# Layer one's twelve weight-pair blocks all by seven products, with low halves and column sums allowed on GpSimd, in a fused attention and two-layer MLP kernel

## The chip, the cores and the metric

The kernel runs on one core of a Trainium2 chip. The metric is device time in microseconds (us) of one execution; lower is better. The kernel before took 608.57 us (median of 3 runs, 606.79 to 608.82).

## The reference

Everything is float32. An attention (batch 2, 8 heads, 768 positions, head size 64; each position sees the last 96 positions and the first 8, with a bias that falls linearly with distance) gives 1536 tokens of 512 numbers. Two MLP layers follow:

```
x = attention(q, k, v)                       # 1536 x 512
h = x @ w_in;  r = max(h, 0);  g = s*r*r + b;  x = g @ w_out      # layer one, 512 -> 2048 -> 512
h = x @ w_in2; r = max(h, 0);  g = r*r;        out = g @ w_out2   # layer two
```

The weights arrive as 64-bit floats and are decoded on the chip.

## The kernel before, in words

**Precision.** A float32 operand is split into a high half (rounded to the fp32r format, on ScalarE or GpSimd: `whi`, `wsh`, `gh`, `tsh`, `zsh`) and a low half, which is the operand minus its high half (a two-input subtract, on VectorE: `wlo`, `wsl`, `gl`, `tsl`, `zsl`, lines 441, 475, 612, 615, 523). A product takes three matmuls: high by high, high by low, low by high.

**Blocks.** The hidden width 2048 is cut into 16 chunks of 128 in each layer. The first four chunks of layer one (`h` L695, `y` L774, 256 tokens at a time) are interleaved with the attention. All other chunks are worked in pairs (a, a+1): six pairs in layer one (4 to 14) and eight in layer two (16 to 30), each for two token halves tp of 768, so twelve blocks in layer one and sixteen in layer two. A pair of weight chunks by a token half is a 2 x 2 block product. Either it is done plainly (`plain` L549: 4 results x 4 row blocks x 3 = 48 matmuls of 384 columns), or by seven products in Winograd's form (`product` L538: 7 x 2 x 3 = 42 matmuls). `PLAIN` lists the blocks done plainly: pairs 4 and 6, both halves.

**What seven products need beside the matmuls.** For each pair of weight chunks, four sums of weight blocks (`ws` L458) and their split (`wshi`, `wslo` L475). For each token half, four column sums T1 to T4 for two row blocks kt (`tsum1` L517 in layer one, `tsum` L504 in layer two), each split by `tsplit` (high L221 or L225, low L523). They are worked one after the other, T3, T1, T2, T4 for kt 0 and then for kt 1, in one buffer of tag `tq`; layer two's use the buffer `m1`, which also holds the copy of a block's first product (`mid`). T1 overwrites a part of X, so it waits until the first four chunks, and the plain blocks, have read it. For each block, VectorE adds the products together: `mid` u2 and u3 (L559) and three `cadd` (L572), from PSUM. The products run in the order of `STAGES`: A11*B11, S2*T2, A12*B21, S3*T3, S1*T1, A22*T4, S4*B22.

**From layer one to layer two.** Layer one's output is summed in `acc` (`flush` L781, `flush2` L664). Because g is made as sign(s) times its value (`sg`), `acc` is multiplied by `sg` at the end by four ScalarE instructions a token half (`flush2` part 1, through `copy_r` L221), and only then split and summed in columns for layer two.

**Order.** `order` lists every task with the engines that may run it, a planned duration, what it depends on, its place in the rings of buffers and a due time `key`, to which `SHIFT` adds. `Plan.run` then walks through time and gives each engine the ready task with the least key. That fixes the instruction order of every engine and the choice of engine where several are allowed ("DVX" is a VectorE task that also uses the port shared with GpSimd). On the chip every engine works through its own queue in that order and waits on semaphores. Where TensorE has no ready task before the first `h`, the plan puts in a small matmul on zeros (`warm` L324).

In layer two the first product of a block waits for all eight column sums and the three splits of the token half, in layer one for all eight column sums (`dt`, added to stage 0 alone).

Of the kernel before, what the change touches and what calls it, by code (L numbers as in the profile page):

```python
# [19 lines left out]
P = 128  # L20
# [10 lines left out]
PLAIN = ((4, 0), (6, 0), (4, 1), (6, 1))  # L31
# [27 lines left out]
def decoded(a):  # L59
# [9 lines left out]
SHIFT = {('at', 0, 0): -17.4, ('at', 2, 0): 83.2, ('at', 2, 3): -18.5, ('at', 3, 0): 18.1, ('at', 6, 0): -32.5,  # L69
    ('at', 8, 0): -19.9, ('at', 8, 1): -18.7, ('cadd', 16, 0, 1, 0): 13.9, ('cadd', 24, 0, 1, 1): 64, ('cadd', 8, 0,  # L70
# [28 lines left out]
    0): -49.2, ('qk', 9, 0): -21.3, ('relu', 0, 0): 113.3, ('relu', 0, 256): 15.4, ('relu', 1, 0): -19.6, ('relu',  # L99
# [21 lines left out]
class Plan:  # L121
# [13 lines left out]
    def run(self, lat, patience):  # L135
# [92 lines left out]
class Fast:  # L228
# [269 lines left out]
    def tsum(self, tp, kt, step):  # L498
        b = [self.part(tp, x)[:, kt] for x in range(4)]
        if step % 3 == 0:  # L500
            self.T["t", tp, kt] = self.tm.tile([P, SB], F32, tag="m1", name=f"t{step}_{tp}_{kt}")
# [852 lines left out]
```

## Time and profile before

| what | value |
|---|---|
| median of 3 runs | 608.57 us (606.79 to 608.82) |
| the profiled execution's own time | 606.85 us |
| its span, first to last instruction | 605.1 us |
| granted TensorE clock, mean | 0.999 |

How to read the profile: PE is TensorE's matmuls, PEld its weight loads, DVE VectorE, ACT ScalarE, POOL GpSimd. A matmul's recorded length includes its run through the array, so matmuls overlap; the distance from one start to the next is what one costs. A row of the timeline has: start us, length us, engine, line, operation, output<-input, shapes, how many were merged, and in brackets the idle time before it with what ended it. A row of the instruction groups has: count, then busy us and mean ns of one, then idle time before them with what ended it. A row of the windows has: the stretch, its length, then busy us and count for PE, PEld, DVE, ACT and POOL, the granted clock, the DMA share and GB/s. A row of the waits has: total us, times, longest.

### The profile page before, as it was taken

How to read it: one execution, taken by the hardware profiler on the slowest of the kernel's cores; microseconds unless marked ns; L12 is line 12 of the kernel's file. 1: busy time of each engine (PE TensorE's matmuls, PEld its weight loads, DVE VectorE, ACT ScalarE, POOL GpSimd, SP SyncE). 2: the span in 40 equal slices, each digit the busy share in tenths (PEclk: the TensorE clock that was granted, in tenths of full speed). 3: DMA queues.
4: the chain of work that ended last, by engine and by line, in shares of the span. 5: the costliest groups of instructions: out<-in, count | busy, mean ns of one | idle time of the engine just before them, and what ended most of it. 6: DMA issues, size and time to landing. Idle time of an engine off the chain costs nothing.

```text
span 605.1 us, 10174 instructions
## 1 busy us (share of the span) xinstructions
PE 591.4 (98%) x3705; PEld 533.9 (88%) x3705; DVE 496.8 (82%) x1115; ACT 354.5 (59%) x774; POOL 113.7 (19%) x187
## 2 busy tenths in 40 slices
PE   8999999999999999999999899999999999999995
PEld 5788898999999999999999788899899999899984
DVE  7999898877999799987989999989587978774452
ACT  7999897756754445544667585655354645434330
POOL 5464432101112111111201012213010111000000
PEclk9999999999999999999999999999999999999999
DMA  7775641022321200312130302241222122000023
GB/s 283 286 268 182 218 157 39 3 96 73 111 70 36 80 26 1 110 61 74 51 124 1 104 2 70 69 140 35 70 69 90 51 69 71 35 1 1 0 106 109
DMA packets 14889, 52.11 MB, mean 86 GB/s; under 512 B 1904, under 2 KB 2160, under 8 KB 14832
## 3 DMA queue, kind: packets, MB, share of 16 engines
q1 hardware_dynamic: 14832, 51.39, 25.2%
q8 instruction: 31, 0.51, 0.3%
q14 instruction: 26, 0.21, 0.1%
HBM read 48.24 MB, written 3.15 MB: 85 GB/s over the span
## 4 chain that ended last, share of the span: by engine, by line


## 5 line engine op out<-in xcount | busy, mean ns | idle before, releaser
L538 PE MATMUL h<-xh,u 128*128 128x384 f32 x384 | 111.7, 337 | 1.2 <-ACT m L221 1.2
L641 PE MATMUL yy<-u,gh 128*128 128x512 f32 x360 | 111.8, 392 | 0.0
L635 PE MATMUL yy<-gh,u 128*128 128x512 f32 (+1 forms) x384 | 97.7, 337 | 0.2 <-ACT gh L605 0.2
L538 PE MATMUL h<-th,u 128*128 128x384 f32 x288 | 85.6, 338 | 0.0
L641 PEld LDWEIGHTS yy<-u,gh 128*128 128x128 f32 x360 | 67.2, 188 | 11.8
L635 PEld LDWEIGHTS yy<-gh,u 128*128 128x128 f32 x384 | 66.8, 189 | 8.5 <-ACT gh L605 0.5
L225 POOL TENSOR_SCALAR u<-st 128x512 fp32r<-128x512 f32 (+1 forms) x47 | 35.2, 749 | 202.4 <-PE h L538 58.7
L538 PEld LDWEIGHTS h<-xh,u 128*128 128x128 f32 x384 | 70.5, 188 | 2.6 <-ACT m L221 1.5
L641 PE MATMUL yy<-u,gl 128*128 128x512 f32 x180 | 70.4, 391 | 0.7 <-DVE gl L615 0.7
L635 PE MATMUL yy<-gl,u 128*128 128x512 f32 (+1 forms) x192 | 64.9, 338 | 1.8 <-DVE gl L612 1.8
L538 PE MATMUL h<-xl,u 128*128 128x384 f32 x192 | 64.6, 337 | 0.0
L538 PEld LDWEIGHTS h<-th,u 128*128 128x128 f32 x288 | 53.1, 188 | 1.9 <-DVE u L559 0.4
L221 ACT ACTIVATE u<-st 128x512 fp32r<-128x512 f32 (+1 forms) x41 | 26.2, 639 | 44.6 <-PE h L538 13.4
L221 ACT ACTIVATE st<-st 128x512 f32<-128x512 f32 x64 | 42.8, 676 | 11.7 <-DMA st<-in_moe_w_in_dram 8.0
L52 DVE SCALAR_TENSOR_TENSOR st<-st 128x512 int32<-128x512 int32 x64 | 46.1, 723 | 3.7 <-ACT st L221 0.9
L538 PE MATMUL h<-tl,u 128*128 128x384 f32 x144 | 48.5, 337 | 0.0
L375 ACT ACTIVATE sn<-sn,nm 128x256 f32<-128x256 f32 (+1 forms) x96 | 46.0, 483 | 1.4 <-DVE nm L367 1.3
L55 DVE SCALAR_TENSOR_TENSOR st<-st 128x512 int32<-128x512 int32 x64 | 44.8, 700 | 0.9
L594 ACT ACTIVATE r<-r 128x384 f32<-128x384 f32 x64 | 33.6, 526 | 13.6 <-DVE r L589 9.0
L635 PEld LDWEIGHTS yy<-gl,u 128*128 128x128 f32 x192 | 36.3, 189 | 5.9 <-DVE gl L612 2.1
L641 PEld LDWEIGHTS yy<-u,gl 128*128 128x128 f32 x180 | 33.8, 188 | 8.5 <-DVE gl L615 1.1
L585 ACT ACTIVATE u<-u 128x384 f32<-128x384 f32 x32 | 16.7, 522 | 37.6 <-DVE u L572 37.5
(153 smaller groups left out, 1308.9 us busy)
## 6 DMA issues: line engine op xcount, KB each, us to landing
st<-in_moe_w_in_dram SPq DMA_DIRECT2D x32, 512.0 KB, 3.9
st<-in_moe_w_out_dram SPq DMA_DIRECT2D x32, 512.0 KB, 3.6
q<-in_qk_dram SPq DMA_DIRECT2D x10, 768.0 KB, 5.0
v<-in_v_dram SPq DMA_DIRECT2D x10, 512.0 KB, 4.6
out_dram<-acc SPq DMA_DIRECT2D x11, 256.0 KB, 2.3
q<-in_qk_dram SPq DMA_DIRECT2D x2, 512.0 KB, 5.0
v<-in_v_dram SPq DMA_DIRECT2D x2, 256.0 KB, 6.0
out_dram<-acc SPq DMA_DIRECT2D x2, 128.0 KB, 3.1
```

Source lines behind the costliest of these rows:

```text
L52: nc.vector.scalar_tensor_tensor(out=lo, in0=hi, scalar=3, in1=lo, op0=ALU.logical_shift_left, op1=ALU.bitwise_or)
L55: nc.vector.scalar_tensor_tensor(out=lo, in0=hi, scalar=-(1 << 31), in1=lo, op0=ALU.bitwise_and, op1=ALU.bitwise_or)
L221: nc.scalar.activation(out=out, in_=in_, func=AF.Copy, scale=scale)
L225: nc.gpsimd.tensor_scalar(out=out, in0=in_, scalar1=scale, scalar2=0.0, op0=ALU.mult, op1=ALU.add)
L375: self.nc.scalar.activation(out=sn[:, x], in_=sn[:, x], func=AF.Exp, scale=-1.0, bias=self.nm[:, n, h:h + 1], accum_out=self.rs[:, n, h:h ...
L538: self.nc.tensor.matmul(ps, p, q, start=first and kt == 0 and x == 0, stop=kt == 1 and x == 2, skip_group_check=not first)
L585: nc.scalar.activation(out=r, in_=h, func=AF.Relu, scale=rt)
L594: nc.scalar.activation(out=r, in_=r, func=AF.Square)
L635: self.nc.tensor.matmul(yj, p[:, js], q[:, lo:hi], start=first and x == 0 and not (side and j % 2), stop=last and x == 2 and not (side and ...
L641: self.nc.tensor.matmul(y[m], p[:, ms], q, start=first and x == 0, stop=last and x == 2)
```

## The change

All blocks of layer one go by seven products (`PLAIN` is empty). The low halves of weights, of column sums and of layer two's g, and layer two's column sums themselves, may run on GpSimd beside VectorE. The sign is applied where layer one's results leave PSUM (`flush`, `flush2`), and the eight ScalarE instructions on `acc` go. Each product waits for the one column sum or split that it reads. Layer two's column sums use the buffer `tq`. The token half that is needed first gets its sums first. `SHIFT` has other values throughout, and a table `PIN` of 202 entries fixes a task's engine; the plan adds a cost when TensorE turns between kinds of work, and some planned durations change. The diff, with both tables cut to a few entries:

```diff
-PLAIN = ((4, 0), (6, 0), (4, 1), (6, 1))
+PLAIN = ()
...
-SHIFT = {('at', 0, 0): -17.4, ('at', 2, 0): 83.2, ('at', 2, 3): -18.5, ('at', 3, 0): 18.1, ('at', 6, 0): -32.5,
...
+SHIFT = {('at', 10, 3): 21.4, ('at', 2, 1): 59.4, ('at', 4, 0): 46.1, ('at', 4, 3): -15.5, ('at', 6, 1): -4.2,
...
+    ('lq', 2): -536.5, ('lq', 3): -435.9, ('lq', 4): -186.5, ('lq', 7): -193.6, ('lw', 0, 0): -5.9,
...
+PIN = {('at', 0, 0): 'ACT', ('at', 2, 0): 'ACT', ('at', 2, 1): 'DVE', ('at', 2, 3): 'DVE', ('at', 4, 0): 'ACT',
...
+TURN = ((0.0, 0.09, 0.18, 0.08), (0.095, 0.0, 0.095, 0.095), (0.095, 0.095, 0.0, 0.095), (-0.08, 0.09, 0.09, 0.0))
+KIND = {"qk": 1, "pv": 2, "tr": 3}
...
                     free[e] = now + engs[e]
+                    if e == "PE":
+                        k = KIND.get(self.tasks[t][0][0], 0)
+                        free[e] += TURN[kind][k]
+                        kind = k
...
-    def tsum(self, tp, kt, step):
+    def tsum(self, tp, kt, step, e):
...
-            self.T["t", tp, kt] = self.tm.tile([P, SB], F32, tag="m1", name=f"t{step}_{tp}_{kt}")
+            self.T["t", tp, kt] = self.tq.tile([P, SB], F32, tag="tq", name=f"t{step}_{tp}_{kt}")
...
-        self.nc.vector.tensor_tensor(out=t, in0=x, in1=y, op=ALU.subtract)
+        getattr(self.nc, e).tensor_tensor(out=t, in0=x, in1=y, op=ALU.subtract)
...
-            self.nc.vector.tensor_tensor(out=l, in0=t, in1=h.bitcast(F32), op=ALU.subtract)
+            getattr(self.nc, e).tensor_tensor(out=l, in0=t, in1=h.bitcast(F32), op=ALU.subtract)
...
-            nc.vector.tensor_tensor(out=gl, in0=r, in1=gh.bitcast(F32), op=ALU.subtract)
+            getattr(nc, e).tensor_tensor(out=gl, in0=r, in1=gh.bitcast(F32), op=ALU.subtract)
...
-                nc.vector.tensor_tensor(out=a, in0=y, in1=a, op=ALU.add)
-            elif part == 1:
-                a = accT[:, j, t0:t0 + TB]
-                copy_r(nc, e, a, a, self.sg)
+                nc.vector.scalar_tensor_tensor(out=a, in0=y, scalar=self.sg, in1=a, op0=ALU.mult, op1=ALU.add)
...
-            self.nc.vector.tensor_tensor(out=a, in0=y, in1=a, op=ALU.add)
-        else:
-            copy_r(self.nc, e, a, y)
+            self.nc.vector.scalar_tensor_tensor(out=a, in0=y, scalar=self.sg, in1=a, op0=ALU.mult, op1=ALU.add)
+        else:
+            copy_r(self.nc, e, a, y, self.sg)
...
+        if name in PIN:
+            engs = {e: d for e, d in engs.items() if e.replace("DVX", "DVE") == PIN[name]}
...
-        add(("wlo", w, i), "DVX:0.61", lambda e: f.wlo(w, i, e, v), [("whi", w, i)] + late(w, i, "l"), key,
+        add(("wlo", w, i), "DVX:0.61 POOL:1.25", lambda e: f.wlo(w, i, e, v), [("whi", w, i)] + late(w, i, "l"), key,
...
-            add(("wsl", what, a), "DVX:0.34" if small else "DVX:0.61",
+            add(("wsl", what, a), "DVX:0.34 POOL:0.75" if small else "DVX:0.61 POOL:1.25",
...
-    for tp in range(2):
+    tps = sorted(range(2), key=lambda tp: min((t for _, a, x, t in quads if x == tp and not plain(a, x)), default=0.0))
+    for tp in tps:
...
-                add(("zsl",) + v + (x,), "DVX:0.51", lambda e, v=v, x=x: f.tsplit(*v, x, 1, e),
+                add(("zsl",) + v + (x,), "DVX:0.51 POOL:1.0", lambda e, v=v, x=x: f.tsplit(*v, x, 1, e),
...
-        if not one:
-            dt = [("tsl", tp, kt, x) for kt in range(2) for x in range(4)] + [("xl", "x", tp, j) for j in (0, 2, 3)]
-        elif plain(a, tp):
-            dt = ["second"]
-        else:
-            dt = [("zsl", tp, kt, x) for kt in range(2) for x in range(4)]
         wino = not plain(a, tp)
+        tl = lambda x: [("zsl" if one else "tsl", tp, kt, x) for kt in range(2)]
+        xl = lambda j: ["second"] if one else [("xl", "x", tp, j)]
+        dt = (xl(0), tl(1), xl(2), tl(3), tl(0), tl(2), xl(3))
...
-                    [prev] + [("wsl", x, a) for x in need[s]] + extra[s] + dt * (s == 0), tm + 1.05 * s,
+                    [prev] + [("wsl", x, a) for x in need[s]] + extra[s] + dt[s], tm + 1.05 * s,
...
-            add(("gl",) + v, "DVX:0.56" if one else "DVX:0.49", lambda e, v=v: f.act(*v, "gl", e), [("gh",) + v], k,
+            add(("gl",) + v, "DVX:0.56" if one else "DVX:0.49 POOL:1.0", lambda e, v=v: f.act(*v, "gl", e), [("gh",) + v], k,
...
-            for j in range(4):
-                add(("sg", tp, j), "ACT:0.85", lambda e, g=g, tp=tp, j=j: f.flush2(g, tp, j, 1, e),
-                    [last[j], last[4 + j // 2]], k)
...
-                    add(("ts",) + v + (x,), "DVX:0.49", lambda e, v=v, x=x: f.tsum(*v, x),
+                    add(("ts",) + v + (x,), "DVX:0.49 POOL:1.0", lambda e, v=v, x=x: f.tsum(*v, x, e),
-                        sgn(kt) + [("tsl",) + v + (x - 1,)] * (x > 0) + [("tsl", tp, 0, 3)] * (kt > 0), k,
-                        acq=[("m1", "t") + v + (x,)] * new)
+                        acq=[("tq", "t") + v + (x,)] * new)
```

Of the 202 entries of `PIN`, 30 put a low half or a column sum on GpSimd (8 `wsl`, 7 `gl`, 7 `wlo`, 5 `zsl`, 1 `tsl`, 2 `ts`); tasks without an entry are left to the plan.

## Rows read from the trace of the kernel before

**Rows 1.** The page: the span, and busy time of each engine.
```profile
span 605.1 us, 10174 instructions
PE 591.4 (98%) x3705; PEld 533.9 (88%) x3705; DVE 496.8 (82%) x1115; ACT 354.5 (59%) x774; POOL 113.7 (19%) x187
```

**Rows 2.** The waits of PE, longest in total.
```profile
PE yy L635 <- DVE gl L612: 1.8, 1, 1.8
...
PE h L538 <- ACT m L221: 1.2, 1, 1.2
...
PE yy L641 <- DVE gl L615: 0.7, 1, 0.7
```

**Rows 3.** Windows: busy time by engine before, in and after layer one.
```profile
100.00:145.00 45.00, 44.91 (x421) 42.62 (x421) 35.88 (x104) 29.43 (x76) 7.50 (x13) 1.00 0.10 36
145.00:320.00 175.00, 175.00 (x1020) 164.15 (x1019) 154.80 (x282) 97.06 (x174) 24.64 (x33) 1.00 0.22 70
320.00:385.00 65.00, 61.12 (x321) 54.32 (x320) 63.31 (x117) 44.97 (x79) 9.91 (x13) 1.00 0.16 49
```

**Rows 4.** PE's timeline: plain blocks (L549), y (L774), seven products (L538).
```profile
145.22 0.34 PE L549 MATMUL h<-xh,u 128*128 128x384 f32 x1
...
153.66 0.28 PE L774 MATMUL y<-gh,u 128*128 128x256 f32 x1
...
157.96 0.34 PE L549 MATMUL h<-xh,u 128*128 128x384 f32 x1
...
162.12 0.28 PE L774 MATMUL y<-gh,u 128*128 128x256 f32 x1
...
163.55 0.34 PE L549 MATMUL h<-xh,u 128*128 128x384 f32 x1
...
304.09 0.34 PE L538 MATMUL h<-xh,u 128*128 128x384 f32 x1
...
308.26 0.39 PE L635 MATMUL yy<-gh,u 128*128 128x512 f32 x1
```

**Rows 5.** Instruction groups by line: what the change adds, takes out or moves.
```profile
L475 DVE TENSOR_TENSOR u<-st,u 128x512 fp32r<-128x512 f32 (+1 forms) x48 | 31.1, 665 | 4.5 <-PE yy L641 3.2 <-PE yy L635 0.9 <-ACT u L221 0.4
...
L441 DVE TENSOR_TENSOR u<-st,u 128x512 fp32r<-128x512 f32 x40 | 27.6, 693 | 5.5 <-PE yy L635 2.5 <-POOL u L225 2.0 <-ACT u L221 0.7
L572 DVE TENSOR_TENSOR u<-h,u 128x384 f32<-128x384 f32 x48 | 26.5, 553 | 13.1 <-PE h L538 12.8
L559 DVE TENSOR_TENSOR u<-h,m 128x384 f32<-128x384 f32 x48 | 26.5, 552 | 7.5 <-PE h L538 5.6 <-ACT st L221 1.7
...
L458 DVE TENSOR_TENSOR st<-st,st 128x256 f32<-128x256 f32 x36 | 16.4, 478 | 0.3
...
L221 ACT ACTIVATE acc<-acc,sg 128x768 f32<-128x768 f32 x8 | 7.2, 927 | 0.0
```

**Rows 6.** DVE's timeline: first instructions of column sums, layer one, first token half.
```profile
128.27 0.55 DVE L517 TENSOR_TENSOR tq<-xh 128x384 f32<-128x384 f32 x1
...
132.71 0.56 DVE L517 TENSOR_TENSOR tq<-xh 128x384 f32<-128x384 f32 x1
...
179.43 0.56 DVE L517 TENSOR_TENSOR tq<-xh 128x384 f32<-128x384 f32 x1
...
183.65 0.54 DVE L517 TENSOR_TENSOR tq<-xh 128x384 f32<-128x384 f32 x1
...
187.73 0.56 DVE L517 TENSOR_TENSOR tq<-xh,tq 128x384 f32<-128x384 f32 x1
...
190.74 0.55 DVE L517 TENSOR_TENSOR tq<-xh,tq 128x384 f32<-128x384 f32 x1
```

**Rows 7.** Timeline of POOL and of DVE where they meet.
```profile
334.85 0.98 POOL L225 TENSOR_SCALAR u<-st 128x512 fp32r<-128x512 f32 x1 [4.16 <-PE yy L635]
...
335.23 1.01 DVE L504 TENSOR_TENSOR t<-acc 128x384 f32<-128x384 f32 x1
```

**Rows 8.** Instruction group: the small matmuls on zeros in the first 25 us.
```profile
L324 PE MATMUL warm<-idle 128*128 128x256 bf16 x48 | 7.0, 283 | 0.0
```

More of the change, by code (lines that the diff above doesn't have):

```diff
@@ new lines @@
+SHIFT = {('at', 10, 3): 21.4, ('at', 2, 1): 59.4, ('at', 4, 0): 46.1, ('at', 4, 3): -15.5, ('at', 6, 1): -4.2,
+    ('at', 8, 2): 153.6, ('cadd', 12, 0, 1, 0): 116.6, ('cadd', 18, 0, 0, 1): 106.2, ('cadd', 18, 0, 1, 0): 42.9,
[19 rows of a table added]
+    ('norm', 11, 1): -157.2, ('norm', 11, 2): 52.7, ('norm', 3, 1): 18, ('norm', 5, 0): 14.2, ('norm', 8, 3): -3.9,
[5 rows of a table added]
+    0, 1024): 41.9, ('relu', 12, 0, 0, 1): 49.2, ('relu', 3, 1024): 156.6, ('relu', 3, 512): -24, ('relu', 4, 0, 0,
[3 rows of a table added]
+    9, 1): 82.4, ('ts', 0, 0, 2): -8.9, ('tsl', 0, 0, 1): -1.3, ('ttr', 3, 2): -31.7, ('ttr', 5, 0): 30.5, ('u2',
+    18, 1): 55.6, ('u2', 24, 0): 34.6, ('u2', 6, 0): -22.5, ('u2', 8, 1): 117.3, ('whi', 1, 0): 87.9, ('whi', 12,
+    1): 189.2, ('whi', 21, 1): 34.2, ('whi', 4, 1): -32.7, ('wlo', 19, 1): 28.4, ('wlo', 25, 1): 5.5, ('wlo', 26,
[3 rows of a table added]
+    ('wsh', 'S34', 6): 4.6, ('wsl', 'A1', 10): -72.6, ('wsl', 'A1', 20): 130.3, ('wsl', 'A1', 24): -1.6, ('wsl',
[9 rows of a table added]
@@ L146, in run @@
         held = {"DVE": 0.0, "POOL": 0.0}
+        kind = 0
         self.busy = dict.fromkeys(ready, 0.0)
@@ L823, in order @@
     plan.fill, plan.until = lambda: f.warm(0), ("h", 0, 0)
-    add("n", "SP:0.47", lambda e: None, key=-1000.0, dma=0.06)
+    add("n", "SP:1.2", lambda e: None, key=-1000.0, dma=0.06)
     add("nd0", "POOL:2.1", lambda e: f.consts(0), key=-60.0)
@@ L847, in order @@
                     dq.append(("tr", m, grp(m, mf)[0]))
-                add(("qk",) + u, {"PE": 1.07 if two else 1.17}, lambda e, u=u: f.qk(*u), dq, t, acq=[("a", "s", x) + u for x in range(2)],
+                add(("qk",) + u, {"PE": 0.97 if two else 1.1}, lambda e, u=u: f.qk(*u), dq, t, acq=[("a", "s", x) + u for x in range(2)],
                     rel=[("q", n)] * (hf or not two))
@@ L861, in order @@
                     lambda e, w=w: f.norm(*w, e), [("rs",) + u], t - 1)
-                add(("tr",) + w, {"PE": 0.45}, lambda e, w=w: f.tr(*w), [("norm",) + w], t - 2,
+                add(("tr",) + w, {"PE": 0.438}, lambda e, w=w: f.tr(*w), [("norm",) + w], t - 2,
                     acq=[("a", "t") + w], rel=[("sN",) + w])
@@ L867, in order @@
         t = vt[n, 1] + (cfg["att"] if two else -500.0)
-        add(("pv", n), {"PE": 1.9 if two else 1.1}, lambda e, n=n: f.pv(n), [("at", n, g) for g in grp(n, None)] + [("lv", n)],
+        add(("pv", n), {"PE": 1.8 if two else 1.0}, lambda e, n=n: f.pv(n), [("at", n, g) for g in grp(n, None)] + [("lv", n)],
             t - 3, acq=[("a", "o", n)], rel=[("at", n, g) for g in grp(n, None)] + [("v", n)])
@@ L976, in order @@
         tm, fin = t + cfg["moe"], lo == NT - 256
-        add(("h",) + u, {"PE": 1.44}, lambda e, u=u: f.h(*u, u[1] + 256), dh, tm, acq=[("h",) + u],
+        add(("h",) + u, {"PE": 1.43}, lambda e, u=u: f.h(*u, u[1] + 256), dh, tm, acq=[("h",) + u],
             rel=[slot(w, 0, x) for x in "hl"] * fin)
@@ L985, in order @@
         add(("gl",) + u, "DVX:0.42", lambda e, u=u: f.glo(*u, u[1] + 256), [("gh",) + u], t, rel=[("r",) + u])
-        add(("y",) + u, {"PE": 1.45}, lambda e, u=u, new=new, end=end: f.y(*u, new, end),
+        add(("y",) + u, {"PE": 1.435}, lambda e, u=u, new=new, end=end: f.y(*u, new, end),
             [("gl",) + u, ("wlo", w, 1)] + ([("y",) + before] if before else []) + last * new, tm + cfg["ylag"],
@@ L993, in order @@
                 more = lo in done
-                add(last[j], "DVE:0.6" if more else "DVE:0.6 ACT:0.48",
-                    lambda e, lo=lo, j=j, more=more: f.flush(lo, j, more, e), [("y",) + u], t)
+                add(last[j], "DVE:0.67" if more else "DVE:0.6 ACT:0.5",
+                    lambda e, lo=lo, j=j, more=more: f.flush(lo, j, more, e), [("y",) + u, ("root", 0)], t)
             done.add(lo)
     fin = {a: tp for _, a, tp, _ in quads}
-    for tp in range(2):
+    tps = sorted(range(2), key=lambda tp: min((t for _, a, x, t in quads if x == tp and not plain(a, x)), default=0.0))
+    for tp in tps:
         d0 = ["second"] + [("h", w, lo) for w in range(NF) for lo in range(tp * TB, tp * TB + TB, 256)]
@@ L1117, in order @@
                 df += [("xl", "x", k, x) for k in range(2) for x in (0, 2, 3)]
-            add(name, "DVE:0.6 ACT:0.48" if g[0] == NCH else "DVE:0.6",
+            add(name, "DVE:0.6 ACT:0.48" if g[0] == NCH else "DVE:0.67" if one else "DVE:0.6",
                 lambda e, g=g, tp=tp, j=j: f.flush2(g, tp, j, 0, e), df, tc + span + cfg["tk"])
@@ L1125, in order @@
             k = tc + span + cfg["tk"]
-            for j in range(4):
-                add(("sg", tp, j), "ACT:0.85", lambda e, g=g, tp=tp, j=j: f.flush2(g, tp, j, 1, e),
-                    [last[j], last[4 + j // 2]], k)
-            sgn = lambda kt: [("sg", tp, kt), ("sg", tp, kt + 2)]
             for j in (0, 2, 3):
+                r, c = divmod(j, 2)
                 add(("xh", "x", tp, j), "ACT:0.75", lambda e, g=g, tp=tp, j=j: f.flush2(g, tp, j, 2, e),
-                    [("sg", tp, j // 2 * 2), ("sg", tp, j // 2 * 2 + 1)], k)
-                add(("xl", "x", tp, j), "DVX:1.0", lambda e, g=g, tp=tp, j=j: f.flush2(g, tp, j, 3, e),
+                    [last[2 * r], last[2 * r + 1]] + [last[4 + r]] * c, k)
+                add(("xl", "x", tp, j), "DVX:1.03", lambda e, g=g, tp=tp, j=j: f.flush2(g, tp, j, 3, e),
                     [("xh", "x", tp, j)], k)
@@ L1138, in order @@
                     new = x % 3 == 0
[L1139 to L1141 removed]
+                    add(("ts",) + v + (x,), "DVX:0.49 POOL:1.0", lambda e, v=v, x=x: f.tsum(*v, x, e),
+                        [[last[kt], last[4]], [last[kt + 2], last[5]], [], []][x] + [("tsl",) + v + (x - 1,)] * (x > 0) +
+                        [("tsl", tp, 0, 3)] * (kt > 0), k,
+                        acq=[("tq", "t") + v + (x,)] * new)
                     add(("tsh",) + v + (x,), "ACT:0.44 POOL:0.6", lambda e, v=v, x=x: f.tsplit(*v, x, 0, e),
                         [("ts",) + v + (x,)], k)
[L1144 to L1145 removed]
+                    add(("tsl",) + v + (x,), "DVX:0.51 POOL:1.0", lambda e, v=v, x=x: f.tsplit(*v, x, 1, e),
+                        [("tsh",) + v + (x,)], k, rel=[("tq", "t") + v + (x // 3 * 3,)] * (x > 1))
     add("check", "DVE:2.0", lambda e: f.check(), ["second", ("relu", NF - 1, NT - 256)], use[6],
```

57 lines of the change are left out of this document (40 added, 17 removed), and 83 rows, old and new, of tables (PIN, SHIFT).

## The prediction

> **What bounds the kernel now.** I read the page's busy times first: TensorE is busy for 591.4 of 605.1 us, VectorE for 496.8, GpSimd for 113.7 [rows 1]. TensorE sets the time; the reader should see also that VectorE comes next and that GpSimd has room. Busy matmuls overlap, so I then took two other views. The list of TensorE's waits names three that matter, 1.8 + 1.2 + 0.7 = 3.7 us, all behind VectorE or ScalarE [rows 2]. The windows say where: TensorE is busy in all of 145 to 320 us (layer one's blocks), and loses 3.9 us in 320 to 385, the passage from layer one to layer two, where VectorE is busy for 63.3 of 65 us [rows 3]. In layer one VectorE works 154.8 of 175 us, just before it 35.9 of 45. So two things can shorten the kernel: fewer matmuls anywhere, and an earlier end of VectorE's work in the passage. One thing can lengthen it: more work on VectorE in layer one.
>
> The profiled execution took 606.85 us, 1.7 above its span and 1.7 (0.28%) below the median of the three runs, inside their spread. The sum starts from 606.85; 0.3%, about 1.8 us, is what a measurement of this kernel can tell from no change.
>
> **Part 1, four blocks by seven products.** A plain block's 48 matmuls run from 145.22 to 153.66, 0.176 us each; 24 matmuls of seven-product work run from 304.09 to 308.26, 0.174 each [rows 4]. A block loses six matmuls, so 4 x 6 x 0.174 = 4.2 us. TensorE has no idle time there to hide this, so it comes off the end in full: **-4.2**.
>
> What it adds goes to VectorE: per block two `mid` and three `cadd` at 0.55, 4 x 5 x 0.55 = 11.0 us; per weight pair four sums at 0.48, 2 x 4 x 0.48 = 3.8; four low halves at 0.665 in place of two at 0.693, 2 x 1.27 = 2.5 [rows 5]. Together 17.3 us. From 100 to 320 us VectorE works 190.7 of 220 [rows 3]; with the addition it would be 208 of 216, so it still fits, by 8 us, without any help. I cost it at nothing; the cover is these 8 us, and what comes late when they are gone is the low half (`gl`) for which `yy` waits, the wait of [rows 2]. High halves and copies for the new weight sums (some 2 to 4 us) go to ScalarE, idle 78 of 175 us there [rows 3].
>
> **Part 2, the column sums come earlier.** Their number stays, but until now the plain blocks ran first. The first sum starts at 128.27, once the attention is done [rows 6], and this floor stays. S2*T2 of the first block needs T1 for both kt, but the sums are made T3, T1, T2, T4, so it needs seven links of the chain. Links with three VectorE instructions took 4.44, 4.22 and 4.08 us to the start of the next, one with two took 3.01 [rows 6]: four at 4.2 and three at 3.0, the last without the gap to its successor (some 2.6), give 25.4, so T1 is there at about 153.7. TensorE's other work: the first block could start at 145.22, four `y` behind it (153.66 to 157.96 and 162.12 to 163.55, 5.7 us) can come first, and A11*B11 needs no sum (6 x 0.174 = 1.0) [rows 4]: enough until 152.0. So **+1.7**. Since TensorE takes its queue in order, all its later matmuls stand behind that wait. The bounds: nothing, if the links keep to their bare instructions or the new order ends the attention earlier; +7.4, if all seven take 4.44.
>
> **Part 3, the passage to layer two.** Eight multiplications by `sg` of 0.927 each leave ScalarE [rows 5], and the eviction multiplies instead, with the same operands plus one number per partition, so VectorE's count stays. A token half's sums no longer stand behind four of them. The column sums leave the buffer `m1`, for which the first product's copy waits (1.2 us of [rows 2]); the first product waits for one split in place of eight sums and three splits; some sums and low halves leave VectorE, on which the `gl` of the other two waits queued. I take 3.2 of the 3.7 us away, **-3.2**; the bounds are 0 (all stays) and 3.9 (the whole loss of the window).
>
> **Part 4, low halves on GpSimd.** No row shows GpSimd with two inputs. The nearest is its one-input split of 128 x 512 in 0.98 us, part of it spent against VectorE [rows 7]; the plan in the diff puts 1.25 on a low half. I take 1.25. Each one frees 0.67 us of VectorE. What it costs VectorE is seen where they meet: a two-input subtract of 128 x 384, 0.55 us elsewhere [rows 6], took 1.01 when it started 0.60 us before the end of GpSimd's split [rows 7]. It lost 0.46, all but 0.14 of what was left. Bounds for one low half: nothing lost, or 1.25 - 0.14 = 1.11. I take 0.45, the loss of that row, since instructions with an input in PSUM ran beside GpSimd's at a mean of 0.55 [rows 5]. Thirty low halves then free 30 x (0.67 - 0.45) = 6.6 us. This moves nothing on TensorE by itself: 0. GpSimd's queue grows by some 38 us of 605, but the high halves it also makes stand behind these longer instructions; whoever reads them waits up to 1.25 us more, and the weights are made well ahead of use.
>
> The Trainium skill, GPSIMD Engine Reference, section 3.1, states about 2.6 cycles an element for two inputs on GpSimd and advises VectorE for such work. An estimate from it is 512 x 2.6 / 1.2 GHz = 1.11 us plus dispatch, so the sum by the page would be that by the plan's 1.25; no run here shows it yet.
>
> **Part 5, the new order.** The loads of attention tiles 2 to 4 move far forward in SP's queue, ahead of weight loads. No transfer is added. In the first 25 us, 48 small matmuls, 7.0 us, fill TensorE's waiting [rows 8]: that bounds a gain; a loss could be as large. I take 0, as every operation of that chain stays. The cost for turning between kinds of work adds no instruction.
>
> **Sum.** 606.85 - 4.2 + 1.7 - 3.2 = 601.15, **601.2 us**, against 606.85, and 0.9 to 1.2% below the runs shown.
>
> **The rivals.** *A, the passage keeps its waits* (another VectorE instruction stands before `gl`): 606.85 - 4.2 + 1.7 = 604.4. For it: VectorE has 1.7 us of room in 65 there, and relief rests on GpSimd. Against: 7.4 us of ScalarE in that very chain go. *B, the first block waits for its sums at the slow pace*: 606.85 - 4.2 - 3.2 + 7.4 = 606.9, no change. For it: all of VectorE's added work begins just there. Against: VectorE has 9 us free from 100 to 145, and nothing fixes the attention's end at 128.
>
> *C, GpSimd stops VectorE, slower.* In layer one, nearly every low half on GpSimd halts a two-input instruction on VectorE for its length: 1.11 lost for 0.67 gained, 0.44 each, 30 x 0.44 = 13.2 us. VectorE's 208 become 221 of 216, 5 us over, and TensorE waits for `gl`; the passage gains nothing: 606.85 - 4.2 + 1.7 + 5 = 609.4, and 0.44 more for each further one. It decides from the point at which six in ten meet this fate (0.67/1.11). For it: the subtract of [rows 7] lost nearly the full remainder. Against: in layer one GpSimd was busy for 24.6 us and TensorE lost nothing [rows 3]; and five in each block's VectorE instructions read PSUM. The Trainium skill, SBUF — State Buffer, section "Who interferes with whom", speaks for C: the port that VectorE and GpSimd share is locked for a whole instruction, a two-input one on VectorE against one on GpSimd that reads SBUF. By that rule the loss is the full remainder, and the row agrees, with 0.46 of 0.60.
>
> *D, the change does not do what it says*: tasks with both engines may still land on VectorE, which is then at 96% in layer one, like the passage now; that ends in A or B.
>
> **Chances and range.** Forecast 0.64, A (with D) 0.14, B 0.10, C 0.12. Faster by over 0.3%: 0.64 + 0.14 = 0.78; within it: B, 0.10; slower: C, 0.12. The forecast's own range is 598 to 604. Downward I add the bounds of parts 2 and 3 (-1.7 and -0.7) and half of the fill (-3.5): about 595.5. Upward the range takes in A and, just, B: 606.7; it leaves out C and tails.
>
> **What would show it.** Right: 1176 matmuls of 384 columns in place of 1200, all on the product's line; the three waits of the passage gone or under 0.5 us together; at about 150 us a wait of TensorE for a low half of T1 under 3 us; VectorE at 92 to 97% from 130 to 320 without TensorE waiting. A wait of 5 us or more at the first block means B, waits for `gl` all over layer one with long subtracts beside GpSimd mean C, waits at 320 to 385 mean A. The prediction would be wrong downward if the first 25 us shrink.

## The result, and the profile after

The changed kernel takes **616.91 us** (median of 4 runs, 616.69 to 617.18) against 608.06 (606.79 to 608.82) for the kernel before: ratio 1.0148, 95% interval 1.0128 to 1.0168. It is 8.9 us slower, where 601.2 was forecast and 595.5 to 606.7 was the range; that is the side of rival C.

The page after, to be held against [rows 1]:

```profile
span 615.3 us, 10202 instructions
PE 594.3 (97%) x3681; PEld 530.7 (86%) x3681; DVE 516.1 (84%) x1031; ACT 356.1 (58%) x784; POOL 245.3 (40%) x293
```

TensorE has its 24 matmuls fewer. VectorE has 84 instructions fewer and is busy 19.3 us *longer*; GpSimd is busy 131.6 us longer. The waits of TensorE after, against [rows 2]:

```profile
PE chkp L842 <- DVE chk L839: 3.4, 1, 3.4
PE h L589 <- DVE u L610: 2.7, 4, 1.3
PE yy L686 <- DVE gl L663: 2.6, 4, 1.2
PE h L589 <- DVE u L623: 2.3, 3, 1.3
...
PE h L743 <- POOL u L492: 0.7, 1, 0.7
```

All but the last stand behind VectorE. `chkp` is the transpose of the kernel's check of its counts, which stands in TensorE's queue just ahead of the first block; `u` of L610 and L623 and `gl` of L663 are a block's recombinations and low halves. The windows after, against [rows 3], and one more around the check:

```profile
100.00:145.00 45.00, 44.38 (x412) 42.05 (x411) 38.02 (x82) 30.12 (x75) 17.43 (x23) 1.00 0.15 48
145.00:320.00 175.00, 167.60 (x960) 154.61 (x959) 161.09 (x266) 96.81 (x176) 64.47 (x64) 0.99 0.22 67
320.00:385.00 65.00, 62.62 (x336) 55.40 (x335) 63.55 (x89) 36.08 (x64) 43.18 (x40) 1.00 0.15 48
```

```profile
140.00:160.00 20.00, 16.52 (x114) 16.14 (x113) 17.33 (x36) 9.35 (x20) 10.07 (x12) 0.91 0.02 7
```

Layer one, where TensorE lost nothing before, now loses 7.4 us. VectorE does fewer instructions there (266 for 282) in more time (161.1 for 154.8 us). The passage still loses 2.4 of 65 us, and the granted clock is down to 0.91 for 20 us around 150.

What GpSimd has taken on is 116 subtractions with two inputs, 144.5 us by my sum over the trace, 1.25 each. Their largest group of one shape:

```profile
L492 POOL TENSOR_TENSOR u<-st,u 128x512 fp32r<-128x512 f32 x24 | 34.1, 1420 | 39.2 <-ACT u L272 33.3 <-DVE st L50 4.9
```

And groups of VectorE after. L52, L55 and L50 unpack the stored weights, and the change touches neither their number nor their shape; L610 reads a matmul's result in PSUM, the memory that matmuls write, while the first three read SBUF, the memory of all other operands:

```profile
L52 DVE SCALAR_TENSOR_TENSOR st<-st 128x512 int32<-128x512 int32 x64 | 56.8, 888 | 3.2
L55 DVE SCALAR_TENSOR_TENSOR st<-st 128x512 int32<-128x512 int32 x64 | 51.0, 799 | 1.0
L50 DVE TENSOR_SCALAR st<-st 128x512 int32<-128x512 int32 x64 | 36.9, 578 | 1.2 <-DMA st<-in_moe_w_in_dram 1.2
...
L610 DVE TENSOR_TENSOR u<-h,m 128x384 f32<-128x384 f32 x56 | 30.8, 550 | 11.1 <-PE h L589 9.8 <-ACT st L272 1.1
```

The first three in the kernel before:

```profile
L52 DVE SCALAR_TENSOR_TENSOR st<-st 128x512 int32<-128x512 int32 x64 | 46.1, 723 | 3.7 <-ACT st L221 0.9
L55 DVE SCALAR_TENSOR_TENSOR st<-st 128x512 int32<-128x512 int32 x64 | 44.8, 700 | 0.9
L50 DVE TENSOR_SCALAR st<-st 128x512 int32<-128x512 int32 x64 | 27.9, 440 | 0.0
```

The same 192 instructions cost 144.7 us instead of 118.8, while L610, with an input in PSUM, keeps the 552 ns of its counterpart in [rows 5]. Sorting the instances after by what ran on GpSimd beside them (at least 0.1 us of overlap; excess over the lower quartile of the line's lengths; worked out from the trace):

```
line, what it reads              nothing       one input     two inputs on GpSimd
L52  two inputs in SBUF       x30  -2 ns     x11  +83 ns    x23  +509 ns
L55  two inputs in SBUF       x36  +4        x12  +40       x16  +419
L50  one input in SBUF        x32  +2        x14  +75       x18  +504
L568 two inputs in SBUF       x24  -2        x3  +104       x13  +658
L610 one of two in PSUM       x39  +6        x6   +6        x11   +4
L715 one of two in PSUM       x17  +1        x6   +3        x13   +1
```

VectorE is halted only beside GpSimd, mostly beside its two-input work, and only where it reads SBUF alone. Below, this is called the lock. Over the whole kernel this excess (instances over 30 ns counted) is 75.2 us after and 14.5 before: 60.7 more, 0.52 for each of the 116.

The order of starting says more than the means do (worked out from the traces before and after, for VectorE's decoding, sums and low halves where they meet one instruction of GpSimd). An instruction of VectorE that starts before GpSimd's loses at most 0.014 us (117 instances). One that starts while GpSimd's is running loses what is left of that less 0.13 to 0.20 us. That holds beside two inputs (52 instances, up to 1.13 us lost) and beside one input (55, up to 0.47 us lost). In 15 more beside one input, over 0.65 us was left and VectorE lost nothing; there GpSimd's instruction ended behind VectorE's. So one rule covers both kinds; GpSimd's two-input instructions keep VectorE standing for longer.

Where TensorE feels it most at once is seen in the timelines of VectorE, of GpSimd and of TensorE after, before the first block (start, length, and in brackets the idle time before):

```profile
143.20 1.44 DVE L52 SCALAR_TENSOR_TENSOR st<-st 128x512 int32<-128x512 int32 x1
...
145.13 1.10 DVE L568 TENSOR_TENSOR tq<-xh 128x384 f32<-128x384 f32 x1
...
150.29 1.53 DVE L568 TENSOR_TENSOR tq<-tq,xl 128x384 f32<-128x384 f32 x1
151.74 0.24 DVE L839 TENSOR_REDUCE chk<-nm 128x1 f32<-128x96 f32 x1
```

```profile
143.07 1.03 POOL L574 TENSOR_TENSOR tl<-tq,th 128x384 fp32r<-128x384 f32 x1 [1.04 <-ACT th L272]
...
145.01 0.80 POOL L526 TENSOR_TENSOR u<-st,u 128x256 fp32r<-128x256 f32 x1
...
149.78 1.62 POOL L526 TENSOR_TENSOR u<-st,u 128x512 fp32r<-128x512 f32 x1 [0.53 <-ACT u L272]
```

```profile
152.13 0.27 PE L842 MATMUL chkp<-ident,chk 128*1 128x128 f32 x1 [3.39 <-DVE chk L839]
```

Three of VectorE's instructions run into one of GpSimd's each; L52 starts 0.90 us before GpSimd's end and loses 0.73 over its 0.71 to 0.72, the one at 150.29 loses 0.97 of 1.11 over its usual 0.56. The check's reduction at 151.74 follows them in VectorE's queue, the transpose follows that, and TensorE's whole queue stands behind the transpose for 3.39 us.

### The profile page after: what moved, and what is told of

The parts are those of the page before. It is cut to its first block, busy times and chain, and to the rows that moved or that the text cites. A ratio compares the mean times of both kernels' runs of the same rounds, so it can differ in the third digit from the quotient of the medians.

```text
span 615.3 us, 10202 instructions
## 1 busy us (share of the span) xinstructions
PE 594.3 (97%) x3681; PEld 530.7 (86%) x3681; DVE 516.1 (84%) x1031; ACT 356.1 (58%) x784; POOL 245.3 (40%) x293
## 4 chain that ended last, share of the span: by engine, by line
## 5 line engine op out<-in xcount | busy, mean ns | idle before, releaser
L589 PE MATMUL h<-xh,u 128*128 128x384 f32 x448 | 130.5, 339 | 1.0 <-DVE u L623 1.0
L589 PE MATMUL h<-th,u 128*128 128x384 f32 x336 | 100.5, 340 | 4.0 <-DVE u L610 2.7
L589 PEld LDWEIGHTS h<-xh,u 128*128 128x128 f32 x448 | 82.5, 188 | 3.2 <-DVE u L623 1.7
L589 PE MATMUL h<-xl,u 128*128 128x384 f32 x224 | 75.6, 337 | 0.0
L589 PEld LDWEIGHTS h<-th,u 128*128 128x128 f32 x336 | 61.9, 188 | 8.6 <-DVE u L610 4.9
L52 DVE SCALAR_TENSOR_TENSOR st<-st 128x512 int32<-128x512 int32 x64 | 56.8, 888 | 3.2
L589 PE MATMUL h<-tl,u 128*128 128x384 f32 x168 | 56.5, 336 | 0.0
L272 ACT ACTIVATE st<-st 128x512 f32<-128x512 f32 x64 | 42.1, 676 | 24.1 <-DMA st<-in_moe_w_in_dram 11.8
L55 DVE SCALAR_TENSOR_TENSOR st<-st 128x512 int32<-128x512 int32 x64 | 51.0, 799 | 1.0
L276 POOL TENSOR_SCALAR u<-st 128x512 fp32r<-128x512 f32 (+1 forms) x40 | 27.9, 698 | 58.8 <-DVE st L55 23.5
L276 POOL TENSOR_SCALAR sn<-sn,rs 128x256 f32<-128x256 f32 (+1 forms) x58 | 28.7, 509 | 56.8 <-DVE rs L432 35.9
L492 POOL TENSOR_TENSOR u<-st,u 128x512 fp32r<-128x512 f32 x24 | 34.1, 1420 | 39.2 <-ACT u L272 33.3
L526 POOL TENSOR_TENSOR u<-st,u 128x512 fp32r<-128x512 f32 (+1 forms) x34 | 41.8, 1236 | 18.1 <-ACT u L272 16.9
```

The lines of the kernel that those rows point to most:

```text
L52: nc.vector.scalar_tensor_tensor(out=lo, in0=hi, scalar=3, in1=lo, op0=ALU.logical_shift_left, op1=ALU.bitwise_or)
L55: nc.vector.scalar_tensor_tensor(out=lo, in0=hi, scalar=-(1 << 31), in1=lo, op0=ALU.bitwise_and, op1=ALU.bitwise_or)
L272: nc.scalar.activation(out=out, in_=in_, func=AF.Copy, scale=scale)
L276: nc.gpsimd.tensor_scalar(out=out, in0=in_, scalar1=scale, scalar2=0.0, op0=ALU.mult, op1=ALU.add)
L492: getattr(self.nc, e).tensor_tensor(out=wl, in0=decoded(self.T.pop(("st", w, i))), in1=self.T["wh", w, i].bitcast(F32), op=ALU.subtract)
L526: getattr(self.nc, e).tensor_tensor(out=t, in0=self.wsrc(a, what), in1=self.T[what, "h", a].bitcast(F32), op=ALU.subtract)
```

## The experiments

**Everything on VectorE, the order kept.** The kernel after, its 116 subtractions issued on VectorE at the same places of the order (lines 492, 526, 555, 574, 666):

```
-  getattr(self.nc, e).tensor_tensor(out=l, in0=t, in1=h.bitcast(F32), op=ALU.subtract)
+  self.nc.vector.tensor_tensor(out=l, in0=t, in1=h.bitcast(F32), op=ALU.subtract)
```

> The changed kernel with its order untouched, but all 116 two-input instructions that ran on GpSimd (low halves, column sums) are issued on VectorE at the same place in the order. Theory L (the port shared by GpSimd and VectorE takes back what GpSimd saves): VectorE gets 116 x about 0.58 = 67 us of work back and loses about 60 us of lengthened instructions, so its busy time stays near 516 (510 to 525) and the time stays at 612 to 618. Theory S (GpSimd is merely slow in chains that TensorE waits for, the lock hardly matters): VectorE's busy time rises by 50 or more and the time is above 622, unless the chains gain more. Theory N (GpSimd is a pure loss): below 609.

607.83 us, ratio 0.9995 (0.9979 to 1.0012): 9.1 us below the kernel after. Its page, then VectorE's group L52, then two of TensorE's waits:

```profile
PE 589.3 (97%) x3681; PEld 529.2 (87%) x3681; DVE 511.3 (84%) x1147; ACT 356.3 (59%) x784; POOL 102.2 (17%) x177
```

```profile
L52 DVE SCALAR_TENSOR_TENSOR st<-st 128x512 int32<-128x512 int32 x64 | 45.2, 708 | 2.6
```

```profile
PE h L589 <- DVE u L610: 2.7, 4, 1.1
PE chkp L842 <- DVE chk L839: 2.4, 1, 2.4
```

With 116 instructions *more*, VectorE is busy 4.8 us *less*. Its busy time is the one that theory L expected, the time of the kernel the one of theory N. So GpSimd's share relieved VectorE by less than nothing: it gave back what the 116 cost there, and 4.8/116 = 0.04 us each on top. TensorE still loses time here, 4.6 us in layer one and 2.4 in the 80 us behind it, which bears on part 1 of the prediction:

```profile
145.00:320.00 175.00, 170.37 (x981) 157.55 (x980) 160.40 (x304) 98.83 (x179) 22.53 (x33) 1.00 0.22 70
320.00:400.00 80.00, 77.63 (x407) 69.21 (x407) 78.97 (x150) 48.61 (x89) 14.74 (x18) 1.00 0.18 59
```

**The column sums alone, and the weights alone, on VectorE.** The same edit in lines 555 and 574 only (31 instructions), and in 492 and 526 only (58).

> The changed kernel with its order untouched, but the 31 column sums and their low halves that ran on GpSimd (lines 555 and 574) are issued on VectorE. Theory S (slow links of the column-sum chain): the first block's waits at 150 to 200 us shrink and the time falls by 4 us or more, to 613 or less. Theory L: the links get shorter by about 0.5 us each but VectorE's time hardly changes; the time falls by 1 to 3 us.

> The changed kernel with its order untouched, but the 58 low halves of weights that ran on GpSimd (lines 492 and 526) are issued on VectorE. Nothing that TensorE waits for at once hangs on them. Theory L: long two-input instructions on GpSimd no longer stop VectorE, about 30 of the 75 us of lengthened VectorE instructions go, and the time stays within 2 us or falls by up to 4. Theory S: VectorE gets 58 x 0.67 = 39 us more work and the time rises by 4 us or more.

614.44 us (ratio 1.0095, 1.0074 to 1.0117) and 611.84 (1.0049, 1.0028 to 1.007). So the sums are worth 2.5 us of the 9.1 and the weights 5.1, more than the 4 that theory L allowed them. The 27 `gl` have no run of their own; if the three add up, 1.5 are left for them, about the width of the intervals. The sums and the weights cost 0.08 and 0.09 us apiece; it isn't one unlucky place.

**One input, and none, on GpSimd.** The kernel after with each of the 116 replaced by a copy with one input on GpSimd, or by a fill with zeros (both leave those low halves and sums out of the result):

```
-  getattr(self.nc, e).tensor_tensor(out=l, in0=t, in1=h.bitcast(F32), op=ALU.subtract)
+  copy_r(self.nc, e, l, t)                      (one input)
+  self.nc.gpsimd.memset(l.bitcast(F32), 0.0)    (the other run: none)
```

> The changed kernel, order and engines untouched, but each of the 116 two-input subtracts on GpSimd is replaced by a one-input copy of its minuend (so those low halves and sums are left out of the result). GpSimd holds the shared port for some 0.65 us in place of 1.25. Theory L (VectorE stands still for as long as GpSimd reads): VectorE's lengthening falls from 75 to 35 to 45 us, its busy time to about 480, and the time to 606 or less, below the kernel with all halves on VectorE (607.8). Theory S (only the late result counts): about the same, 606 to 610, with VectorE's lengthening still above 60.

> The same places, but GpSimd only writes zeros there and reads nothing (these low halves and sums are left out of the result, and what they would have waited for is no longer waited for). Theory L, in the form that it is GpSimd's reading that stops two-input instructions on VectorE: the lengthening falls to the 14 us of the kernels without GpSimd subtracts, VectorE's busy time to about 455, time 602 to 605. If writing alone stops VectorE too, the lengthening stays above 25 us.

597.24 us (ratio 0.9819, 0.9792 to 0.9846) and 597.16 (0.9818, 0.9788 to 0.9847), some 19.7 us below the kernel after, and lower than theory L expected of the fills (602 to 605). The excess of VectorE's lengths, as counted above, goes from 75.2 to 29.4 and to 15.8, against 14.5 before. First the page with copies, then the one with fills:

```profile
PE 587.1 (99%) x3681; PEld 530.2 (89%) x3681; DVE 472.5 (79%) x1031; ACT 355.1 (60%) x784; POOL 179.0 (30%) x293
```

```profile
PE 586.8 (99%) x3681; PEld 530.4 (89%) x3681; DVE 460.2 (77%) x1031; ACT 354.7 (60%) x784; POOL 144.5 (24%) x293
```

But these instructions are also shorter (0.77 and 0.54 us against 1.42 for 128 x 512), and neither waits for the high half, as the copy reads the first operand; so a low half that comes late could have been the cost as well.

**As long and as late as in the kernel after, without the second input.** Copy from the high half, for which the subtraction also waits, then a fill of the same place (leaves the same halves and sums out):

```
-  getattr(self.nc, e).tensor_tensor(out=l, in0=t, in1=h.bitcast(F32), op=ALU.subtract)
+  copy_r(self.nc, e, l, h.bitcast(F32))
+  self.nc.gpsimd.memset(l.bitcast(F32), 0.0)
```

> The kernel after, with each of GpSimd's 116 two-input subtractions replaced by two instructions on GpSimd that take about as long together: a copy with one input, made from the later operand (the high half), so that the dependence stays, and a fill of the same place with zeros (those halves and sums are left out of the result). It separates the lock from the length: the runs with one-input copies and with fills were also shorter on GpSimd (0.77 and 0.54 us against 1.42 for 128 x 512), so a late low half could have been the cost rather than a halted VectorE. Theory, the lock: VectorE's lengthening stays about 30 us and the time within 3 us of the run with one-input copies, 596 to 601. Rival, the length (a low half that comes 0.6 us later keeps TensorE waiting): 607 to 617, with the waits of the kernel after on TensorE although VectorE's instructions keep their usual length.

598.64 us (ratio 0.9844, 0.9826 to 0.9861), within 1.5 us of the short copies. In turn its page, the group L52, the windows, and the check's first reduction in VectorE's timeline:

```profile
PE 587.4 (98%) x3681; PEld 530.1 (89%) x3681; DVE 473.0 (79%) x1031; ACT 355.1 (60%) x784; POOL 229.1 (38%) x409
```

```profile
L52 DVE SCALAR_TENSOR_TENSOR st<-st 128x512 int32<-128x512 int32 x64 | 47.1, 738 | 3.8 <-ACT st L272 0.7
```

```profile
145.00:320.00 175.00, 174.43 (x1012) 162.53 (x1011) 154.67 (x278) 102.30 (x185) 63.76 (x103) 1.00 0.22 73
320.00:400.00 80.00, 80.00 (x424) 73.18 (x423) 69.39 (x117) 49.07 (x92) 46.53 (x82) 1.00 0.22 73
```

```profile
146.65 0.24 DVE L859 TENSOR_REDUCE chk<-nm 128x1 f32<-128x96 f32 x1
```

GpSimd is busy 229.1 us against 245.3 after, and 63.76 against 64.47 in layer one: nearly as long, at the same places. VectorE's excess is about 30 us, as with the short copies. The second input is gone, and with it TensorE's losses in layer one and the passage; the check's reduction runs 5.1 us earlier. That settles lock against length: what costs is that VectorE halts, not that GpSimd is slow. The span is 18.7 us shorter, of which TensorE's idle time gives 11.8 (615.3 - 594.3 against 596.6 - 587.4) and its busy time 6.9. The 6.9 are mostly waits too, since a matmul's recorded run reaches into the wait behind it. Counted from start to start instead (behind the first 23.5 us, distances over 0.1 us above the usual 0.12, 0.17 or 0.23 of 256, 384 and 512 columns; worked out from the traces), the waits sum to 20.2 us after and 3.1 here. With everything on VectorE they are 12.5, in the kernel before 6.9.

**The check left out.** The run with everything on VectorE, the check reduced to setting its flag (the check of the counts is left out):

```
-  nc.vector.tensor_reduce(out=t, in_=self.nm.rearrange("p a b -> p (a b)"), op=ALU.max,
...
-  nc.vector.tensor_copy(self.ok, u[:, 0:1])
+  self.nc.vector.memset(self.ok, 1)
```

> The kernel with all low halves and sums on VectorE and the order untouched (607.8 us), but the task that checks the mask's parameters writes its flag alone: TensorE's transpose and the ten small VectorE instructions go (the check is left out). There TensorE waited 2.4 us just before layer one's first seven-product block. Theory Q (that wait is a price of its own, set by the check's place in TensorE's queue): 604 to 605.5. Theory W (VectorE is late there whatever stands in TensorE's queue): the wait moves to the next product, 606.5 to 607.8.

606.79 us (ratio 0.9987, 0.9974 to 1.0001): 1.0 less, or 0.5 by the two ratios, of a wait of 2.4; that is theory W. Its longest wait:

```profile
PE h L589 <- DVE u L610: 3.3, 5, 1.4
```

The check is a place at which TensorE meets VectorE's lateness, more than its source. The run with everything on VectorE, which computes everything and meets little of the lock, is as fast as the kernel before, no faster.

**The check moved behind a later block.** In the kernel after:

```
-  add("check", "DVE:2.0", lambda e: f.check(), ["second", ("relu", NF - 1, NT - 256)], use[6],
+  add("check", "DVE:2.0", lambda e: f.check(), ["second", ("relu", NF - 1, NT - 256), ("p", 6, 1, 6)], use[6],
```

and the products of the block (8, 0) wait for it. The expectation speaks of the second block and the third. The blocks of layer one come in the order (4, 0), (6, 0), (4, 1), (6, 1), (8, 0), so the edit puts the check behind the fourth and ahead of the fifth: in the trace `chkp` runs at 223.8 us, behind 168 = 4 x 42 matmuls of the product's line. The same holds for the two later runs that move the check.

> The kernel after with the check moved behind the second seven-product block, before the third (the planner makes a new order with that). Theory, VectorE's lengthened instructions set the time: the 3.4 us wait at the check's transpose goes, and most of it comes back at the first block's low halves, so 614 to 617. Rival, the place of the check is the cost: the wait and the slower clock behind it go, 609 to 613.

636.88 us (ratio 1.0459, 1.0435 to 1.0483): outside both expectations, 20 us slower than the kernel after. TensorE's waits, then the windows:

```profile
PE h L589 <- DVE u L610: 10.7, 7, 4.5
PE h L589 <- DVE u L623: 5.4, 4, 2.9
```

```profile
145.00:320.00 175.00, 161.43 (x896) 146.79 (x894) 154.96 (x260) 87.15 (x157) 62.42 (x59) 0.97 0.19 61
320.00:400.00 80.00, 70.02 (x369) 62.70 (x370) 69.88 (x101) 39.10 (x69) 36.96 (x37) 0.96 0.17 53
...
170.00:175.00 5.00, 5.00 (x16) 4.52 (x16) 4.63 (x10) 2.98 (x6) 0.84 (x1) 0.53 0.19 74
```

The planner made another order from the check's old place on. The tables of the diff (`SHIFT`, `PIN`) were not made for it; there are longer waits, and after them a granted clock of 0.53, near the lower of the two levels, in the last window. So this run says nothing on the place of the check. It suggests that a table belongs to one order, which is taken up below.

**A plan without GpSimd for low halves.** The kernel after, the option `POOL:` struck from the low halves and sums and their pins ignored, the check as in the last run:

```
-  "DVX:0.51 POOL:1.0"
+  "DVX:0.51"
```

> The kernel after, but the planner may not give low halves or column sums to GpSimd (so it plans their 0.34 to 0.61 us on VectorE, where the earlier run changed the engine behind the planner's back), and the check stands between the second and third block. Theory: VectorE has room for all of it, so 604 to 609, near the run that had them on VectorE in the old order. Rival, the order made for GpSimd was already as good as any with VectorE: 607 to 609. If the order is fragile, as in the run of the kernel before with seven-product blocks alone, 615 to 640.

637.38 us (ratio 1.048, 1.0451 to 1.0509), the case of a fragile order. TensorE loses 9.9 of the 175 us of layer one and 8.5 of the 80 us behind it.

**Parts of the change on the kernel before.** Seven products in all blocks alone (`PLAIN = ()`); the sign in the evictions and the waits for the own sum alone (diff as in the change, plain blocks kept); both, with the check moved behind the fourth block:

```
-PLAIN = ((4, 0), (6, 0), (4, 1), (6, 1))
+PLAIN = ()
```

> The kernel before with all twelve blocks of layer one by seven products and nothing else (the planner orders anew; low halves stay on VectorE, a block's first product waits for all eight column sums). The step of the prediction (24 matmuls less, VectorE's 17 us more fit): 603 to 605 plus a wait of 2 to 8 us before the first block, so 604 to 612. Theory V (layer one's VectorE cannot carry the additions): 612 or more, with TensorE waiting for VectorE all along 150 to 320 us.

> The kernel before with part 3 alone: the sign in the evictions, each product waiting for its own column sum, layer two's sums in the buffer of layer one's; plain blocks stay, nothing is allowed on GpSimd. The prediction's step: 3.2 us of the passage's waits go, so 603 to 605. Rival A (the passage keeps its waits, since VectorE is busy throughout it): 606 to 609. The planner orders anew, which can add 1 or 2 us elsewhere.

> The kernel before with the twelve blocks by seven products, the sign in the evictions and the wait for the own column sum, the check behind the second block, nothing on GpSimd and the planner's own order from the old shifts. The seven products alone gave 640.4. Theory, what those 32 us were is the old order's misfit (shifts and waits found for other work): sign and per-product waits take back only the passage's part, 615 to 630. Rival, they were the eight sums and three splits that the first product of each token half waited for: 603 to 610, as with the low halves on VectorE in the new order.

640.42 us (ratio 1.0522, 1.0498 to 1.0547), 610.2 (1.0039, 1.0023 to 1.0055) and 634.61 (1.0421, 1.0381 to 1.046). Two of TensorE's waits with the seven products alone, then two with the sign and the waits alone:

```profile
PE h L538 <- ACT m L221: 6.8, 4, 5.6
PE yy L635 <- POOL gh L609: 6.1, 3, 2.9
```

```profile
PE h L538 <- DVE u L559: 2.5, 4, 0.7
PE h L538 <- DVE u L572: 2.2, 3, 1.1
```

The second kernel no longer waits for `m` at the passage, as part 3 said, but for recombinations on VectorE instead. In the third the wait for `m` is down to 0.3 us, and only 5.8 of the first kernel's 32 us with it, so the eight sums ahead of the first product were not what those 32 were. All four kernels planned anew with seven products in every block lie between 634 and 641 us, with GpSimd or without, whichever tables they have; the kernel after, in the order that its tables were made for, is 18 to 24 below them. A part of that is the clock: it was granted at 0.977 to 0.984 on the mean there against 0.996 after, which over 636 us is an estimated 8 to 12 us at most. A new plan alone doesn't cost so much, as the kernel with the sign and the waits was planned anew too and lost 0.4%. That the tables are the reason is argued from this and not shown; new ones were not made.

## Why the prediction was wrong

**The step that failed first is part 4**, "Thirty low halves then free 30 x (0.67 - 0.45) = 6.6 us. This moves nothing on TensorE by itself: 0." *The count*: 30 was read off the pinned tasks; tasks with both engines and no pin also chose GpSimd, and there were 116. *The price* of 1.25 us on GpSimd was right, and the loss of 0.45 close to the measured 0.52. The bound of 1.11 for one low half is near the longest halt, 1.13. *What it frees* was not 0.67 a piece net of 0.45: put back on VectorE, the 116 make it busy 4.8 us less, so a piece freed about 0.48 (0.52 - 0.04). *The effect on TensorE* was not 0 but 9.1 us, the distance between 616.91 and 607.83. For layer one and the passage hang on VectorE, and the halted instructions lie in both.

**A second step failed, in part 1**: VectorE's 17.3 us more, costed "at nothing" as they fit by 8 us. With everything on VectorE TensorE loses 4.6 us in layer one and 2.4 behind it, where the sum left 1.7 and 0.7; in the same order with VectorE relieved of the 116 (598.64 us run) it loses 0.6 and nothing. With everything on it VectorE is busy for 160.4 of the 175 us, 92%, the low end of the 92 to 97% at which no wait was expected. These 4.6 us more are the larger part of the 6.6 between 607.83 and the forecast; the median of the kernel before beside those runs, 608.61, lies 1.8 above the 606.85 from which the sum starts.

**Rival C had the mechanism**: halts in layer one, waits behind VectorE all over it, and a passage that gains nothing. Its price was too high. At 0.44 for each further one, 86 beyond its thirty would give 609.4 + 37.8 = 647; the net loss to VectorE was 0.04 each, and 609.4 came near only since too few pieces met too high a price. The rule cited for it from the Trainium skill (SBUF — State Buffer, "Who interferes with whom") agrees with the trace: GpSimd that reads nothing leaves VectorE alone (15.8 us of excess against 14.5 before), and instructions with an input in PSUM aren't touched (+1 to +6 ns). The "full remainder" that the prediction drew from it is borne out, but for 0.13 to 0.20 us, by the L52 at 143.20 and the L568 at 150.29, which lost 0.73 of 0.90 and 0.97 of 1.11. The prediction weighed against C that TensorE lost nothing beside 24.6 us of GpSimd in layer one. Those were instructions with one input, which halt VectorE for 0.04 to 0.10 us on the mean in the table above and for 0.47 at most; [rows 7], with 0.46, was one of their longest. The row of layer one was of another kind than what was to be judged by it.

**Part 1, -4.2: right for TensorE.** 1176 matmuls of 384 columns ran on the product's line, at a median distance of 174 ns. They come off in full: TensorE's waits from start to start grow by 13.3 us (20.2 - 6.9) and the slower clock adds 1.0; less 4.2 that is 10.1, and the span grew by 10.2.

**Part 2, +1.7: its bounds held, but not its mechanism.** TensorE waits 3.4 us just before the first block, inside 0 to +7.4; for the check, which follows the sums' chain in VectorE's queue and which the step didn't name. ("T1 is there at about 153.7" means T2, for which S2*T2 waits.) The column sums start earlier than the floor of 128.27 [rows 6], as the attention ends earlier in the new order:

```profile
122.12 1.12 DVE L568 TENSOR_TENSOR tq<-xh 128x384 f32<-128x384 f32 x1
```

The low half of T2 that comes last ends at 153.5 all the same, on GpSimd: the 6 us were spent on the way, and even this first sum is halted, at 1.12 for 0.55. In the 598.64 us run the wait is 0.3, near the lower bound. After the wait there is a price that the step left out. `y` (L822) by single matmuls, before and after:

```profile
148.34 0.28 PE L822 MATMUL y<-gl,u 128*128 128x256 f32 x1
148.46 0.28 PE L822 MATMUL y<-gh,u 128*128 128x256 f32 x1
...
153.78 0.42 PE L822 MATMUL y<-gh,u 128*128 128x256 f32 x1
154.00 0.42 PE L822 MATMUL y<-gl,u 128*128 128x256 f32 x1
```

They follow one another at 0.12 us before and 0.22 behind the wait; the granted clock, full until 150, is 0.77 from 150 to 155 and full again from 160, and the 3.4 us without work are what came before it fell. TensorE didn't wait for T2 at all, as its low half was there at 153.5 and S2*T2 starts at 156.2, behind `y`.

**Part 3, -3.2: didn't come.** The wait for `m` went, as forecast, and others took its place. The waits from 320 to 400 us after:

```profile
PE h L589 <- DVE u L623: 1.3, 1, 1.3
PE h L589 <- DVE u L610: 1.3, 2, 0.7
PE yy L686 <- DVE gl L663: 1.0, 2, 0.7
```

They make 3.6 us, where [rows 2] had 3.7. The step rested on low halves leaving VectorE; VectorE was busy 63.31 of 65 us there before and 63.55 after. Where it is truly relieved (598.64 us run) the window to 400 loses nothing: the far bound of the term, -3.9. The sign had a price too: the eviction with it takes 741 ns against 680, 36 x 0.06 = 2.2 us of VectorE.

**Part 5, 0: right for the start**, the only place it priced (TensorE busy 37.2 of the first 40 us, 36.9 before). It said nothing of the order behind them.

**The sum without the failed steps**: 606.85 - 4.2 + 0 - 3.9 = 598.75, and the kernel in which GpSimd works nearly as long but halts VectorE little took 598.64. The bounds of parts 2 and 3 are picked afterwards, so that the two agree to 0.1 us is luck. What it shows is that with VectorE relieved, TensorE loses only 0.6 us from 100 to 400; it is no kernel to use, as it leaves the low halves out. (The recorded range ends at 606.7 and is said to take in B, which comes to 606.9.)

## What to carry to other kernels

Before work is moved to an engine that has room, find out what it takes from the engine it is to relieve: here two-input work on GpSimd gave VectorE back no time at all. A row with shorter instructions of that engine is no measure of it; sort the instances of one unchanged instruction by what runs beside them and by which starts first. Room on an engine's sum over a stretch isn't room where the next engine waits for it: at 92% of layer one VectorE already held TensorE up. And count the moved work in the plan as it comes out, not in the pins.

## What was not expected of the hardware

An instruction of VectorE with one input in SBUF is halted as well: L50 by 504 ns beside a two-input one of GpSimd, as the Trainium skill (SBUF — State Buffer, "Who interferes with whom") allows for `tensor_scalar`, which L50 is; the rival had counted two-input work alone. The time also rises steeply with VectorE's load, in one and the same order of the work:

| what GpSimd does at the 116 places | VectorE busy, us | time, us |
|---|---|---|
| writes zeros | 460.2 | 597.16 |
| one-input copy | 472.5 | 597.24 |
| one-input copy and fill, nearly as long as after | 473.0 | 598.64 |
| nothing, VectorE does all | 511.3 | 607.83 |
| 58 subtractions (sums and `gl`) | 513.4 | 611.84 |
| 85 subtractions (weights and `gl`) | 513.9 | 614.44 |
| 116 subtractions | 516.1 | 616.91 |

From 460 to 473 busy us the kernel loses 0.1 us, or 1.5 where the low halves come nearly as late as after; from 473 to 511 it loses 9.2, and from 511 to 516 again 9.1: the last step is no matter of the sum alone. Which instructions are halted counts, and the runs don't tell these from the others one by one. No version was found that beats the kernel before and computes everything.
